# A maximum over partitions and the lower halves of weights leave GpSimd, in an mLSTM and mixture-of-experts kernel

## The chip, the cores and the metric
The kernel runs on one core of a Trainium2 chip. The time is the device time of one execution in microseconds; lower is better. An execution holds a span, from the first to the last instruction that the profiler records, and a little around it.

## The reference, cut to what matters
Three stages follow each other. The first is an mLSTM, a recurrent attention with gates, for 2 batches of 8 heads, 768 steps and heads of 40. Its output is read as 1536 rows (tokens) of 320 numbers. The second sends each row to two of eight experts and mixes their answers. The third is a two-layer network with an ELU between its layers.

```python
# first stage, for each step t
C = f_stab * C + i_stab * einsum('bhd,bhe->bhde', vt, kt)
y[:, :, t] = sigmoid(o_gate) * einsum('bhde,bhe->bhd', C, qt) / maximum(abs(nq), 1.0)
# second stage, x: (1536, 320)
noisy_logits = x @ w_gate + log1p(exp(x @ w_noise)) * noise
top2, top2_w = the two largest of a row, and their softmax
out[row] += top2_w[k] * (maximum(x[row] @ w1[e], 0.0) @ w2[e])      # w1: 8 x 320 x 1024
# third stage
h = x @ w_in                                                        # 320 x 2048, 64-bit
return where(h > 0, h, exp(minimum(h, 0)) - 1) @ w_out              # 2048 x 320, 64-bit
```

## The kernel before, in words
**Halves.** TensorE works in float16. A float32 number x is split into a high half, x rounded to float16, and a lower half, the rest x - high, also in float16; a product is then the sum of three float16 products (high by high, high by low, low by high). So every weight tile that arrives in float32 is split before use: `split_w` (line 903) makes the high half with `high` (on ScalarE for weights, `wh="A"`) and the lower half with `low`. For `low`, the entry `wl="VG"` allows two ways: one instruction on VectorE (L394), or two on GpSimd, which scale the tile in place (L392) and then subtract (L393). The weights of the last layer arrive as 64-bit numbers; `ffn_piece` (line 1053) puts float32 numbers together from their bits (L1062 to L1070) and then splits them too.

**Stages.** Attention works on 12 tiles of 128 rows, six for each batch (`attention`, `token_rows`); each tile's rows are divided by a power of two near their largest entry, kept as `inv2`, split, and written to memory. The router (`router`) runs once for each batch, with many small steps on VectorE, among them one-hot comparisons (L841, L844, L857) that TensorE sums into lists of rows (L863). For each expert and batch (`expert`), GpSimd gathers the listed rows by indirect transfers (L969), SP's queue transposes them, TensorE multiplies them with the first weights (L933), ScalarE applies the ReLU and makes the high half of the hidden rows (L988), VectorE makes the lower half (L990), and TensorE multiplies with the second weights (L946, L947, L949). Last comes the third stage on six blocks of 256 rows (`last_layer`), whose weights are fetched and split while the experts run.

**The maximum.** The third stage needs one scale for all rows. `scales` (line 1014) takes the largest entry of `inv2` in each partition (L1018), then the maximum over all partitions on GpSimd (L1019), and derives four factors from it (L1022 to L1027), which are used from the third stage on.

**The order.** All work is a list of steps, each with one or more ways (an engine and a price). A planner (`Order.plan`) once put the steps into a sequence by its own prices; the result is the table `ORDER`, which `run` decodes: for each step its number and its way. Each engine then works through its steps in that sequence, in order, and waits where a step's inputs are not there. The prices stand in the calls of `vec`, `act`, `pool` and `te` and don't change what a step does.

Of the kernel before, what the change touches and what calls it, by code (L numbers as in the profile page):

```python
# [5 lines left out]

# [63 lines left out]


ORDER = """
c-jrrzw0{hVF2*w?w<So+}(4(f8WP~gM$GB4i+2?STMzc0Sg8kEI62AieIqc;9$W)iU9)-77V<<V8MbE0|pE@7_i{rV8DVD2LlckELbpLz(D)@BVGVNfB^
>(aDV|4L<tnZ&xruUKpZrPDtHqKPy=O<0(oE%E#MGsA_<zHMWjIn0I~ooU_^X~F_8r^qC<QUUE-JIjDX~jjFS_h4%(m(dPG2QWDktV3^^wfBqFE87);3&k
pl~2N%RR!CdnD-g5Q!EVns|ygB%bka!oj7mJG-(xg#;LA<pCw6sQr{5*KnvGyo#9)Q(7#F)~Mfk$G}M?#UTBC$Hpz+!HtQP9BI1m8Xtmjw+Bv@<{wASt5^
AnS78%>I)pGI<+86)QM<Q74k`*s0-DE9grm&)Bu#J{~{(}Nv_B<)uCQwmwHoI;zGR1DVT!=sKOpqhaa*@eW)r~p;{E6t`r9WtWr1XPV}h(l_Vgw0yVNmEk
TZ`!4o_~1Rn%P)yX@RCx$$t8e{`P_zz@@Y?GL}z%9V=K|QG((Sk$DpbCTmi-bpws1DhKeRzXc_@c&CKuxF^<-iRXzyQWz8&0Va-z9tG5I%_xtkZGWg$ek9
cen!w@I@i|0cX^Um{V~g37d2Zrs2O+OA62#*q||;g(JA4TJ#tus6J`XNoqi@!35^u6h2{`x_~2a=ses|De4Qh=^2Fd3l`y)dc!mo&?B0oPoPAU;1$f_0xs
ciV28eeG5w);)SjBrfQiu?xQ26j2lsFf$`COeGvOz6oSrci_%F<qP7@1yNgv=5X1N>(nJ)cBC+HrXq`#OIouczxf+=uCuEdqO3RmSGAj#CYGpKV7uE}BM1
^RTBX>o0C3v<kvnKA>q!x_vIq?k3`<>G9bahM^UXVP?;C@@2A#&75mmuAOY0cMy9H)pm?z+~tIJLPxGf{8IlX38bmFK*1wxFWNqv-FbL(M!I>e9y0`J#z;  # L80
+I?n9rIhSG=+>%>yCHBC4z?@(4C*}<{?12Wvmd(>;_RQ4T9@po}%$h6EzvVAXh2@A1SELtwh1l>bX3s*R!B&YKTO-!Yp0Bb6p~4*LE3@TKbeV3lEw;*J*e
ttYZcL52GbjE`AK40>V=sJ-y|H=rLSN~!aHAj0iG9#__Q}+lGkam{#FlHb4W`K)*aBM=9_*8S(gUta*XR~gWM9mV@31BMz<1dm`(m$bo9VM}X272LE_3CF
?1usDi+;0j8nPXRV@K?Z|FD1?vyi*f6PDwqY)$AfeP$&5o=5DAEeUV_!vg_vUo7Tsyul8bAyW|+Y*UyB4%-p#{8%uA5o2%;7jgj`<KkSBd+>E(&Q66T>j)
_>#_qVE2`e@bp8T3^2{9qTrMV0Tg)4XCszO`1a}Vyxy|_2`;Q)W+AkPU%;CL+TxvkI_ptuvdLR`RNQCtcu0r4je^9H{c%Hlx4tivC;fak=XuoeO_CdT*-{
|g}@riCn@<MVuhFY+b6%pV0wJO~-V5H~`Fuki_?%2&js*yZD5o&ORVd`X-MC&3Zpd{g{^Fc;EdPCN@2VJl8hR`@~-AtUC5ypR%aVqVOOZ^WS=i&ZhfC;6^
;6<T6jtcg2uFV@A5I21=>Lp+F6)Z~w1Pdtfd@gk1Jr<fA@;!U`UPvIpF#Qzp1;#8a=Al=1>_!d865*f%rCG--$#Pk0*4-rCd;Ui!apcsmy3|gTNYNITA2n
n<hp)^NpltO8=K?{^ac~n3Z35ZMafV$EaEm0Nyt9V33R7SrMYp9OaVg)tO30<Tn+M&L5M~2iwjs)aAD##twMLpC<12jZEsV<Gs7!9PVG#8QFkZMv>3M5W?
pfgHJ7nG758A&avB)6rQl$QR0pd6R}7v0cC#?oEtNW7eouF_4KNExXh4W**|ke<>@!m=R;a$HWyZ)qcD<*781V)B=?lM`}U9!m=)P+I(7%4Inz@8yq_lV9
ks<fW9AW>Qi5k(5x9%0|j5DJ8|nlpY^fR?<(Txs+BiN}sRDRe2#Dq_tF68ggFRN=K<9XO*p7lUqt&DJlh}q?DDPDpjScH08S7P}<6WNCUYgx8<R{QU*#>=
_q66@07LDQ%3Sh8Y(w=B9G<1@}+d;7@jC|`Hg#WUk2(@xyui^EX|a&e2}N|Q(nk%JW_t8BykGo@kO31N4bI1IDs?xB!8(;{gU_6RnFoZF5v<$;vs&?Wn95  # L90
kyu@w%mM>hI|Ft|<YZxgT<)U1bgHp#G+{7!ng}b<i`*?!4$^cLCPWi|q{DnVwjA!_S_X<{KDo`qFPrE5|d{@rWLz&4(g;t)*0-ux(Ug0%1l{Q~jIpwSjv@
K4moLba(c#jWwEnjg<eJNG-tsL<g-|!tHY^WavV}KWGO--p?6{%^pp<ZxX#j2w=)sEWN{s+fYh<oZl?W<$;i38P9OzhyTx>F0*UX7~>^^f?VX4I=%P>*U+
&8kB+z=oF5CTdw9slQSkEzp)~hmUD-Eukf~s+Q8yT2{+x9L{S)t)LaPl2+DE>Q%d`4XvsDRI6!qEvMeqhuYH4D%Af`yQnL5t(H`*Z`6kt=pBvIN1F33ua3
2((baC+Q=4dp{?f`S(t~fYZ*y&>t+j+6)6>RNooYZ^Xz_1LEv~2al3vjr{jTNoFYTp5EvawyKdBjgrfswz>RJ7!A2m+<s6+iv+DAhg)_{I8cKSg->L-1qk
M+HtGEUl7>*`H?qF;=>{$u^DbH+u#>UVvoJ@uFV)*pIH@97`Ct@ri4Hqe35(P`tX8AesF>Bz_!L*r~rjJn>?N5;%>jKC-u*oYZZV`&tPv2i!QH%i9bSQsm
#W=!?0@ue^HjZrpoM&7s@abs=F^t!P%4qC$484Y7^9E`M?GxKKEs+bwGYyRF?>c7z|##%3!S+i)C%(~ey|JJM;RkLYs^rrDNZpO>#8gJunJdB#zGUxh5dz
u4tXmV!D_!vC{nQgOU_RKG{Z;s5d*)|NbZ%oXE88?4rzRZ~k%%zD<Xzt9pxiZ)0#ypyi`7pO;XeP|P*)e`#p3Jj(FbDj=xR_V-X1>jsnKC<8U==NB#jKK5
wklT3`k27#S`#a7VT-eR*3?3lVcqS%_0N`L)vRAw87pgztS@V3{hPJ064ug6T4QTvt*yFsww^ZUysaNvKe8HD(|Xty7dbDx>SAYO?W{l9hO@Qy*1>Y@i*>
X9Yy$^6SL<&5-a1(y>tSW=wgqg?4(zlA?TY=hURKOTcGiyDt`l=|Hnu}2VJGdX-Ej^3hj!YoxdprK*6gF*vDbFP&f7(MV#l4j{r7Iu{?2aOJ-cLg?WujTH
+I5lx@G&z?%M-<XwU7lU2sy))=oNIH{;Cgkv+B-cG~H=zqVI)!x=aiduQjZtkZIT<dmGEQ*qjE-)%X0XYZArs<U?vUfXFpHD};<oVqh~y3WuYITPpTjh%m  # L100
T=FY;II(=v9?CraEweL>CT{#D5?QEPc=a=rxIXYwach1Q<I~V8boV-ksbCWLT=G}?AbDrMWdw37$>Aak`^Kottat-(DRRZ8bcj{s{8_e8`=eS?)++Di`_w
1(J!2JvN?Z(}ryLC72%e%M>_wDW6T(Ea<-qlUJj`wT#;2zzTdvpKn9qhZC4}b@J=s(<(`*ET7bU6=sG4JKpf{YjUDqi4WuNq|BiP!ON_99GphL`kmUe?Qd
1ux+jy?L1OvTn&sdo{1>^}M=Q_WnBPdJV7S_PwU}o%fTV?fp$q52haHBj50`Kk$a$$ZPmtUO8BLWq0hQ{Iu`*fuHm<e%Ak4@bh3F#{8Tg_m^S8FZo5k;+O
rZzw!qD%xn2gKks+^RruSm?YDw<(DgTA&9D1Cf9Uu9kw5Xr{?z~8pZUjd?l1h6zx4P1+FSc~f8%w6jX(Fc;nClP2mj=s{X=;16W_M}&VTw3f9w6hfBA3!;
}gNn?*_eK5^%vF=m#(u2BY8<p2JHx4%Pt*VgU}~!8w=)v*0V(2J>JMEQ3vu2#jDK?1Ddpm*5brf?IG5uE9Nc1gBu<J%fe!4xA8#p8$qjh(a}d1-H-$V_^^
`LMMoa$uJeB!%CP5lR-Yrh1swWcEWpD4Ig1GOa=9@5st!c$VJ8QCt*2!hRyK1upI`$D@4&d{DdHa5srFcB61=l3ZhsPj|x#L>WAYn9Sy={lnydcIm$-4s2
B~RMl=cYQ7LLg?Wht}qgqstn$b8KMxAIBO`>V^eKd>a(LI`m`)Cn;h25wZfp3qfA1x#JZ5^$mXS9iq(JVYg!;t&-yJ#03qH}bKuF)-eMehiG!{0uU@$LTr
y9-B<
"""
# [1293 lines left out]
```

## Time and profile before

| | |
|---|---|
| median of 3 runs | 490.54 us (489.69 to 492.62) |
| the profiled execution | 491.45 us |
| its span | 489.1 us |
| TensorE busy | 444.3 us (91%) |
| VectorE busy | 380.3 us (78%) |
| ScalarE busy | 312.2 us (64%) |
| GpSimd busy | 164.2 us (34%) |
| mean granted clock of TensorE | 0.963 |

PE is TensorE's matrix products, PEld its weight loads, DVE VectorE, ACT ScalarE, POOL GpSimd, SP the engine whose queue starts most transfers. A letter q behind an engine's name is its sequencer. L933 is line 933 of the kernel. The granted clock is a share of TensorE's full 2.4 GHz. Matrix products overlap, so a busy TensorE need not be at its peak.

### The profile page before, as it was taken

Reading aid. Unit: us, or ns where it says so; the run is one execution under the profiler, and the core shown is the slowest. Engines: PE = TensorE matmul, PEld = TensorE weight load, DVE = VectorE, ACT = ScalarE, POOL = GpSimd, SP = SyncE. Lnnn points to the kernel's source line nnn. Section 1 sums busy time; section 2 is a strip of 40 time slices with the busy share of each in tenths; the row PEclk is TensorE's granted clock in tenths of the full one; section 3 lists DMA queues with packets and bytes.
Section 4 is the critical chain, followed back from the end, with each engine's and each line's share of the span. In section 5 each row is a group of like instructions: output and inputs, shape, how many; then the busy total and the mean of one; then the engine's idle time right before and its main releaser. Section 6 shows DMA issues by size and latency. Waiting matters only on the chain.

```text
span 489.1 us, 10625 instructions
## 1 busy us (share of the span) xinstructions
PE 444.3 (91%) x4091; PEld 374.5 (77%) x4091; DVE 380.3 (78%) x809; ACT 312.2 (64%) x522; POOL 164.2 (34%) x170
## 2 busy tenths in 40 slices
...
GB/s 144 160 142 152 240 147 139 84 220 198 211 274 232 216 243 55 167 239 248 209 222 221 259 209 102 97 102 69 39 40 56 95 15 42 55 0 28 2 28 34
DMA packets 102554, 66.43 MB, mean 136 GB/s; under 512 B 79216, under 2 KB 94112, under 8 KB 102496
## 3 DMA queue, kind: packets, MB, share of 16 engines
...
## 4 chain that ended last, share of the span: by engine, by line
PE 68%; DVE 13%; DMA 9%; issue 4%; ACT 3%; POOL 2%; SPq 1%; ACTq 0%; DVEq 0%; POOLq 0%
PE S L933 28%; PE O L946 9%; PE O L947 9%; PE O L949 8%; PE O L734 5%; DMA sf<-in_moe_w_in 2%; DMA xT<-xg 2%; PE S L667 2%; DVE hidden L990 1%; DVE one L857 1%; PE T L695 1%; PE S L677 1%; DMA sw<-in_moe_w 1%; DVE xr L394 1%; PE T L696 1%
## 5 line engine op out<-in xcount | busy, mean ns | idle before, releaser
L933 PE MATMUL S<-xT,wa 128*128 128x224 f16 (+1 forms) x1024 | 103.8, 260 | 13.8 <-DVE hidden L990 11.3
L933 PEld LDWEIGHTS <-wa 128*128 128x128 f16 x1024 | 95.2, 100 | 18.3 <-DVE hidden L990 8.8
L933 PE MATMUL S<-x3T,fwa 128*128 128x256 f16 x768 | 88.4, 273 | 2.6 <-DMA x3T<-x3r 2.6
L933 PEld LDWEIGHTS <-fwa 128*128 128x128 f16 x768 | 75.1, 98 | 13.0 <-issue 2.9
L946 PE MATMUL O<-wb,hidden 128*128 128x320 f16 (+1 forms) x256 | 75.8, 301 | 2.6 <-DVE yo L373 1.4
L947 PE MATMUL O<-wb,hidden 128*128 128x320 f16 (+1 forms) x256 | 75.7, 301 | 0.0
L949 PE MATMUL O<-wb,hidden 128*128 128x320 f16 (+1 forms) x200 | 60.4, 302 | 0.0
L946 PE MATMUL O<-fwb,gh 128*128 128x320 f16 x192 | 57.4, 299 | 0.0
L947 PE MATMUL O<-fwb,gh 128*128 128x320 f16 x192 | 57.4, 299 | 0.0
L990 DVE SCALAR_TENSOR_TENSOR hidden<-S,hidden 128x128 f16<-128x128 f32 (+2 forms) x92 | 39.7, 456 | 18.6 <-ACT hidden L988 17.4
L1146 DVE SCALAR_TENSOR_TENSOR ex<-ex,th 128x512 f32<-128x512 f32 x48 | 33.2, 691 | 22.6 <-ACT ex L1144 12.4
L969 POOL DMA_INDIRECT xg<-x_rows,table x32 | 36.7, 1145 | 38.2 <-DMA xT<-xg 21.1
L988 ACT ACTIVATE hidden<-S 128x448 f16<-128x448 f32 (+1 forms) x64 | 31.6, 512 | 16.1 <-PE S L933 13.6
L1145 ACT ACTIVATE re<-S,sca 128x512 f32<-128x512 f32 x48 | 33.0, 688 | 8.8 <-DVE gl__5584 L394 3.0
L1144 ACT ACTIVATE ex<-S,sca 128x512 f32<-128x512 f32 x48 | 32.7, 687 | 9.1 <-PE S L933 5.0
L1143 ACT ACTIVATE th<-S,sca 128x512 f32<-128x512 f32 x48 | 32.8, 687 | 8.9 <-PE S L933 8.9
...
L1147 DVE SCALAR_TENSOR_TENSOR re<-ex,re 128x512 f32<-128x512 f32 x48 | 34.0, 711 | 2.6 <-ACT re L1145 0.6
L947 PEld LDWEIGHTS <-hidden 128*128 128x128 f16 (+1 forms) x256 | 27.1, 106 | 9.8 <-issue 2.8
L946 PEld LDWEIGHTS <-hidden 128*128 128x128 f16 (+1 forms) x256 | 27.1, 106 | 7.5 <-DVE yo L1002 0.4
L383 ACT ACTIVATE gh<-re,sca 128x512 f16<-128x512 f32 x30 | 21.7, 724 | 17.2 <-DVE re L1147 17.2
L392 POOL TENSOR_SCALAR sw<-sw 128x640 f32<-128x640 f32 (+2 forms) x16 | 18.4, 1147 | 38.5 <-ACT wb L383 21.0
...
## 6 DMA issues: line engine op xcount, KB each, us to landing
...
```

Of the source, the lines that this page charges most:

```text
L933: PE.matmul(acc, wa[:, r, w, f * P:(f + 1) * P], xT[:, j, :n], start=(i == 0), stop=(i == 7))
L946: PE.matmul(o, a, wb[:, 0, f % FB], start=(f == 0), stop=False)
L947: PE.matmul(o, a, wb[:, 1, f % FB], start=False, stop=(not b and f == last))
L949: PE.matmul(o, b[0], wb[:, 0, f % FB], start=False, stop=(f == last))
L969: do([("G", 1.1, lambda: G.indirect_dma_start(out=xg()[:n], out_offset=None, in_=(x_all if hf else x_rows[0]())[:, :], in_offset=bass.Indi ...
L988: act(2 * cap, lambda: A.activation(hi(0, cap), src(0, cap), AF.Relu), [ph], [hid[f]])
L990: vec(2 * n, lambda x=x, n0=n0, n=n: V.scalar_tensor_tensor(hi(x, n), src(n0, n), 0.0, hi(n0, n), op0=OP.max, op1=OP.subtract), [ph, hid[f ...
L1143: act(512, lambda: A.activation(th(), pf(), AF.Tanh, scale=sca()[:, 2:3]), [pf, sca], [th], "exp", 1)
L1144: act(512, lambda: A.activation(ex(), pf(), AF.Exp, scale=sca()[:, 1:2]), [pf, sca], [ex], "exp", 1)
L1145: act(512, lambda: A.activation(re(), pf(), AF.Relu, scale=sca()[:, 1:2]), [pf, sca], [re], m=1)
L1146: vec(512, lambda: V.scalar_tensor_tensor(ex(), ex(), 1.0, th(), op0=OP.add, op1=OP.mult), [ex, th], [ex], port=True)
L1147: vec(512, lambda: V.scalar_tensor_tensor(re(), ex(), 0.0, re(), op0=OP.min, op1=OP.add), [ex, re], [re], port=True)
```

## The change
Three edits. The maximum over partitions is no longer one GpSimd instruction: TensorE transposes the column of 128 numbers into one row, VectorE takes the row's maximum, TensorE spreads it over the partitions by a product with a row of ones, and VectorE copies it out. The two intermediate results use the two places of memory tag T, which attention's transposes use before. The lower halves of weights have VectorE as their only way. In the planner's price of attention's float32 head products, the product with the state counts 2 x 128 columns instead of 128. The table is new.

```diff
-    kq="A", yo="VA", wh="A", hv="VA", wl="VG", q3l="V")
+    kq="A", yo="VA", wh="A", hv="VA", wl="V", q3l="V")
...
 ORDER = """
-c-jrrzw0{hVF2*w?w<So+}(4(f8WP~gM$GB4i+2?STMzc0Sg8kEI62AieIqc;9$W)iU9)-77V<<V8MbE0|pE@7_i{rV8DVD2LlckELbpLz(D)@BVGVNfB^
...
+c-jrtJIeyyfdJq$_cQnV%$b=p^BS<QFkoR}zz<xourOd@VPU|+1q-uSSQzjF0~Qt*2HeGf0SgNY0|pFO7;wP_7YtY!aKV6u1Pd1|TyWw2VE6eI4*)dK00a
...
+    def ps_f():
+        return buf(lambda: psum, [P, 512], F32, "T", 2, turns=False)
...
-        n, cols = ((3 + (c > 0)) * H, P) if halves else (H, 4 * P + P * (c > 0))
+        n, cols = ((3 + (c > 0)) * H, P) if halves else (H, 4 * P + 2 * P * (c > 0))
...
-        mb = Buf(lambda: None)
+        mb, mt_ = Buf(lambda: None), Buf(lambda: None)
+        m2 = route.tile([P, 1], F32, name="m2")
+        pm, pb = ps_f(), ps_f()
         vec(12, lambda: V.tensor_reduce(m1, inv2(), axis=AX.X, op=OP.max), [inv2], [mb])
-        pool(1000, lambda: G.partition_all_reduce(smax(), m1, P, bass_isa.ReduceOp.max), [mb], [smax])
+        te(1, 4 * P, lambda: PE.transpose(pm()[:1, :P], m1, id32()), [mb], [pm])
+        vec(P, lambda: V.tensor_reduce(m2[:1], pm()[:1, :P], axis=AX.X, op=OP.max), [pm], [mt_])
+        te(1, P, lambda: PE.matmul(pb()[:, :1], ones32()[:1, :], m2[:1], start=True, stop=True), [mt_], [pb])
+        vec(1, lambda: V.tensor_copy(smax(), pb()[:, :1]), [pb], [smax])
```

Decoded, the two tables compare as follows. The steps rise from 1995 to 1998: VectorE's from 772 to 796, TensorE's from 348 to 350; ScalarE keeps 517 and SP's queue 224; GpSimd's fall from 134 to 111. Twenty-two lower halves of weights move from GpSimd to VectorE, 16 of expert weights and 6 of the last layer's. Of the last layer's roundings, 17 move from ScalarE to VectorE and 8 the other way; of the copies of experts' results, 10 move from VectorE to ScalarE and 6 the other way; three multiplies of last-layer weights move from VectorE to GpSimd. The sequence of experts and batches on TensorE is the same, but the steps of neighbours interleave in another way, and nearly every step stands at another place. In the new table the transpose comes right behind the first product step of expert 3, batch 0; VectorE's maximum 107 VectorE steps behind the step that feeds the transpose; the product that spreads it 46 TensorE steps behind the transpose, among expert 5; the copy among expert 7.

## Rows read from the trace of the kernel before

**Rows 1.** The page's head and busy time: us, share of the span, instructions.
```profile
span 489.1 us, 10625 instructions
...
PE 444.3 (91%) x4091; PEld 374.5 (77%) x4091; DVE 380.3 (78%) x809; ACT 312.2 (64%) x522; POOL 164.2 (34%) x170
```
**Rows 2.** Busy us by stretch, then clock, DMA share, GB/s; experts and last layer.
```profile
130.00:305.00 175.00, 159.15 (x1402) 137.42 (x1400) 140.57 (x258) 100.06 (x178) 67.92 (x59) 0.97 0.81 207
...
321.00:484.00 163.00, 162.24 (x1344) 131.43 (x1344) 121.70 (x204) 112.80 (x189) 23.52 (x25) 1.00 0.16 40
```
**Rows 3.** The chain that ended last, around and behind the maximum: start, us, what.
```profile
184.79 7.03 issue
191.82 1.26 POOL nm L378
...
203.64 2.87 POOL wb L393
...
207.04 5.79 DMA sf<-in_moe_w_in
```
**Rows 4.** Instructions of the maximum's line: min/median/max ns, first and last start.
```profile
L1019 POOLq MODIFY_POOL_CONFIG  x2: 13/13/13, 177.5 to 177.5; - x2
L1019 POOL PARTITION_ALL_REDUCE smax<-m x1: 378/378/378, 184.3 to 184.3; - x1
```
**Rows 5.** Waits from 176 to 200 us: total us, times, longest.
```profile
DVE hidden L990 <- ACT hidden L988: 11.3, 1, 11.3
ACT fwa L383 <- POOL nm L378: 11.1, 1, 11.1
...
POOL smax L1019 <- DMA sw<-in_moe_w: 6.8, 1, 6.8
```
**Rows 6.** TensorE's waits over the whole run, the longest.
```profile
PE S L933 <- DVE hidden L990: 11.3, 5, 8.0
```
**Rows 7.** Busy us by stretch, as rows 2, behind the maximum.
```profile
192.00:200.00 8.00, 5.17 (x25) 3.70 (x26) 5.47 (x8) 5.82 (x9) 6.75 (x6) 0.50 0.22 55
208.00:220.00 12.00, 8.94 (x83) 7.50 (x82) 10.12 (x22) 5.75 (x11) 3.51 (x3) 1.00 1.13 241
```
**Rows 8.** Instructions of two lines near to the new ones, as rows 4.
```profile
L516 PE MATMUL O<-lf,ones x2: 423/476/529, 8.4 to 8.8; 128*128 128x96 f32 x2
...
L1018 DVE TENSOR_REDUCE m<-inv x1: 150/150/150, 178.0 to 178.0; 128x1 f32<-128x12 f32 x1
```
**Rows 9.** Lower halves of weights on GpSimd and on VectorE, as rows 4.
```profile
L392 POOL TENSOR_SCALAR sw<-sw x16: 737/1037/2437, 65.2 to 285.7; 128x640 f32<-128x640 f32 x7, 128x1024 f32<-128x1024 f32 x5, 128x960 f32<-128x960 f32 x4
L392 POOL TENSOR_SCALAR nm<-nm x6: 458/536/630, 194.4 to 298.4; 128x320 f32<-128x320 f32 x5, 128x512 f32<-128x512 f32 x1
...
L394 DVE SCALAR_TENSOR_TENSOR wa<-sw,wa x19: 1208/1218/3149, 64.5 to 279.3; 128x1024 f16<-128x1024 f32 x19
L394 DVE SCALAR_TENSOR_TENSOR wb<-sw,wb x13: 821/1153/1937, 89.3 to 285.0; 128x960 f16<-128x960 f32 x12, 128x640 f16<-128x640 f32 x1
...
L394 DVE SCALAR_TENSOR_TENSOR fwb<-nm,fwb x11: 481/491/493, 219.7 to 306.9; 128x320 f16<-128x320 f32 x11
```
**Rows 10.** Busy us by stretch, as rows 2, where the router's steps fill VectorE.
```profile
64.00:76.00 12.00, 6.84 (x81) 6.08 (x81) 12.00 (x22) 9.78 (x15) 8.28 (x6) 0.78 0.59 147
94.00:104.00 10.00, 6.77 (x89) 6.04 (x88) 9.80 (x24) 5.69 (x9) 8.59 (x8) 0.87 0.76 166
113.00:122.00 9.00, 5.87 (x61) 4.57 (x59) 8.69 (x15) 4.65 (x6) 5.44 (x4) 0.99 0.68 173
```
**Rows 11.** VectorE instructions there: busy us and mean ns, else as rows 4.
```profile
L857 DVE TENSOR_TENSOR one<-minus,bs 128x512 f16<-128x512 f16 x6 | 7.6, 1326 | 0.0
...
L857 DVE TENSOR_TENSOR one<-minus,bs x6: 678/1072/2489, 70.1 to 120.5; 128x512 f16<-128x512 f16 x6
...
L841 DVE TENSOR_TENSOR rh<-starts,as x3: 348/1186/1564, 65.7 to 114.8; 128x192 f16<-128x192 f32 x3
...
L394 DVE SCALAR_TENSOR_TENSOR xr<-yb,sc,xr x24: 239/468/2026, 30.0 to 103.2; 128x256 f16<-128x256 f32 x12, 128x64 f16<-128x64 f32 x12
```

More of the change, by code (lines that the diff above doesn't have):

```diff
@@ L8 @@
 import concourse.tile as tile
-from concourse import bass_isa, mybir
+from concourse import mybir
 from concourse._compat import with_exitstack
@@ L72 @@
 ORDER = """
-c-jrrzw0{hVF2*w?w<So+}(4(f8WP~gM$GB4i+2?STMzc0Sg8kEI62AieIqc;9$W)iU9)-77V<<V8MbE0|pE@7_i{rV8DVD2LlckELbpLz(D)@BVGVNfB^
[L74 to L107, printed above, removed]
@@ L108 @@
-y9-B<
+c-jrtJIeyyfdJq$_cQnV%$b=p^BS<QFkoR}zz<xourOd@VPU|+1q-uSSQzjF0~Qt*2HeGf0SgNY0|pFO7;wP_7YtY!aKV6u1Pd1|TyWw2VE6eI4*)dK00a
+_1pahzP1u%$#I7opaXb=ga3d#TzHSi%4AVwrXi)ev1Q3rW2BGMoO0NDhHD1Z(zBf7*-L=Ql6Owi<<$bupHJF-VCh$RsxE1(M!WE+ftL}bVbF(o9@BKpLN(
+1;vJ5gM5!Epkna$t*b_a%6^@kZEE^4v8swAv45`+z?wLPwt2mIRuEDlY25v?ujee2RUj%9*6_k07vpj+{i4Ir#b+Wck)5T$P=+4k5qvyP(^A0o@AETl0|X
+`mSl;lQ!nyNoyarMrjkU7ER!c{MgEO!P*d<<M1>rK3w0$rRF!;_YqCsz$S&2SKGcn<P!FO;ev?)DO0}pQF$X=WPu0n9Y7J^Mpc*7i)#)3x0u36{O&ZX5YC
+zHSgQ`*!umClxKtM{OG)kg1`c5yw9$55~xX@?%U&tXfqAaRNJgFAlBF~^l=ZP1!0}~!mSGr9jx<ikt7}clS<bdvyH~K|<({F0ZZ$X23&^>ZOVXDsDL7ci1
@@ new lines @@
+nC{X?5Thk#NMAvRoKhPAm^Yy@BRWne=p;R(p0vfxsTR{@64Z-cP$_y$e=})%LeKdO9VeF5ibBi@Wa%lrrurn!%;+4wr3NHqlGL0YF*_<n<!Q{!nHxw`3wl
+Yf=sk6y#>}7THnXKSbdi36H@#qDOo^7*Jw0X#woF%O$bRSpm@o(WNT299v!SL;7Um$$PT4t|U{-vG=`u^E$IO@{lZORZge6#p6L!U<m<mj=8oOqyum<a}0
+h_P|vuvLMM3NmaGqw#outcPpH^{LTo8Y$mkU{K*>B1q*vm==1Fgu1Rw!jwI1-oN2%o9xDmPv70W(s#qoQtt(cE{61fj+TGZU%Sso;kA%e$Vc>GBJl4cFA5
+qiH)-dX2$231<W%mb_JJk4IiMy6_^jWum`rx7MUZv=F8lbt*||K;Okt2D>D`D8yuM`x8$pAAJ*6!w`QB%hTroCuEkY|Ew|?~T$QM^ZSKaNm@Kz}Ij+KN*b
+;MRPuv!snHq8CA8c8;@OQ4tK;pujxh;F+8*G!ka5W~+U6}%RWA4m@Yq1aJ!9Upnyz?)%&33pWSLEu%o9%Kv?!)%EZ}!PuxfeI!ZXDpA%$s}iAFj(Dd79h7
@@ new lines @@
+E8k&Xe4nidkUR0;9Dp>0uqM2iH#6iUZp4kb4`Xo>oN#;i<~7)32keKp;E)}$2m+xgOgY41I2GpHjH?SBffg{g<f=j(#^8!;2{8c*F)j($Tnf&GZ(b5+!iH
+-IX_$ds;Rf46Pq@Pee8Lxe!w>w1fTwxLOT5O#1x>I7jZX*`pAru62>Zf9K>SuXLClYYfiM(u!cNe{7@y&>m=u=6O33mHZZ9CABIfu!kA(tX<gY?rDDi9IA
+dH2CxDjHaC8mX%m=qJR%uj?0kHjip<Bvj0jElbzPQp!i3Uxj$cKN%I5gU9}tcxA-A!NmZkQ0kSQOt`+u`8a1xwMonLQgCS1+g!_#D!E68{$f`q?6bbFXC0
+ai7oM4$O>n%EM}yaFcITC5C`J_2vhMc&cwF(Ez<Hse2Q}sNN@2YR;3<KOA8T7LvbXIMM;*VwX~CBk|rSuOCKRFF=9`;NJ}vx{ak|LM%qhT3CbzyAZhYI-i
+UcAEfu7qbd<8vpTwM0lFE`KHl(dMlIwCsx=Kyy-^IOHlUh<;YVvKVBi*E-)RoraNxDlJIV&H;vow;%(p&0FmOPLq(omjCEg8u<c_uaFw%n9EGM2k?Paex3
@@ new lines @@
+=^@4BxSW(9vZNrTtR&>P^54=+O380|D{D$sIVfp)F6ZT+q_SL)E6PX4N?-n#ck)xVl$4TCV#-TS@JT+a)ReTcmlyI$DJV$=C>bT8<`i04%0)S^ROFSsmN)
+W5p2|?E%0+c1C)KpNQ8Q{*tt)-Lp){42(pEZ3OD!rXwWPGwqw-H`MJ>sBwW_xGj#^NG+*J>9U%AL*<tU$(fihG|YFQnqJGHCyl&gG_*Gf&T$rEL&^wfV=h
+w4bV$up&|j?`}@#ix0oo?%0sD;H&<Y?PNWR%a@$PSm;DRF`T}o2pl3rEb-|x=`=RP047qp3=_pMNMn*uadS_vszBeYi(_!{ZZK}lKxf-+C%v$MQy1+m9kd
+Rs#;CkDF^kTUe%il)w_IDkt(Tmt)VqFsQ0wB-qJc+SKDd>{-)j4zBbT?+DIE~bM2&lRIDzvr#jVU+DkpFD@9j-rfT}Py3|(MT6?Q?{h%GSmA=t-8qknt>3
+a=oEq!Rv+DY3hXRV=k^^4ZllX^y%G^`=Lsb96H_R`|&Mo;M--BQN}*6&(Re`^E%p=I^Hu4`lcXIfhSU+r6)=`lU7SIn4^(~o*Wx3r-?(zp6kk82ZsuIKfH
@@ new lines @@
+HZe~6$N>6FKkFC0X1?{Ze$@+lMc?UrJ!vfTl=0E0dfJE^2_s`<jhu1N^G3-i7{AoZM#X3tPorp5jhp@}y=F8V&1@ST<F40@rg4E?1Dg+BGFrxOjfL?srpC
+9f89QUhTP89~IxrGu%=|W%#>(g$17l{?&7=v;s#()tM#_8}j4?NCBW|Y6oVhm+1~M|%+8CG{V{2s0qj5DRX3;#FCxbCN=Fq$uISZPSnKduw$;?_e>ug@lv
+U4-<CN!pI-pZRL^JV_c7@1@93Lj>{w5*5qG`nWmoS74=VK&X4+2-eF-+Y^Qt7W#$Z}Vx@th@35;jo(4!rYhz>tTG%xwW#OwKbP!%#tk4idzZmVjv4!b*o{
+Ot(Nt+rxrHa*1{@UTWe-5t+iFL4%WshS${Hj*2~(Nd-H51zLH-#yK1e?pIa#_ZSAeM^|9)9(T4W7b+JnJ(Yjh43)p%4U`lqu9`R*+V0EpNRk1C*YPamR-L
+VID%^q4y`?uD&P1_B-X?JbSMt01`cF*qHLwjtW?B7`<d(5ZozBRF@_ROB!8+&1|?6tkM<Mz(p+hglsr|pk@w9hthG$&#I!ls?1owYCa)xOzx`(Z!rmtAqH
@@ new lines @@
+PR;2%b;oiN4sw!C*MZK!k({|Rbg;8<Qcl{5IU}d({Hrr{;?C0fy|Z%u>};KlGjn!M-g&zPC*$m$ADnOZ?i`(uYoUXK5I_y@<j^igE$8f9oQLyt{_eb-7?R
+wZ^L9G?$ANCnvD}{=&5gSZ%Dcc#x^cv#gquKhH|-)f<z`&${@@nfy&H4e&M%$5n{%&j!Ie<MO`?)pb}McQ4cwMnbvw@7y}1Xs?$z9;+jfWU*d4hOx8rtQ4
+gJAwda19z*K=oX%UieuZ|U}&G%BN&+eUZy=$4$ew|0N@GHBygP{+%nJj$UeDxkl(MYMD4sEf{i33X5(^}HHtprO}81Jp!gH1ht<`@Ppf5BKD*(ZxTzQ#3>
+)G(mGTLko2E|KM%W27UY`+MyMCx_fj+7j#8;bn_4Bh92mMX5JIM{WtoD|BYTK?OEOj6+Psg5cYr<^Y&iJd-`+l;@-WCM|;qVdk;V1efzRk_Of2m%j1Q&^w
+yr{9lVrx^v>SO+jtKT1Sjv}74X*Ed4Kn4Kj+2$r}y%1-rM_lKY4T@`I;{UFaUlXLthIlANipl^Amp3Px)y-?^nEnpYiK{-!J(^zw9^tyjR38zk!>$;s4<0
```

5 lines of the change are left out of this document (added).

## The prediction
> **What bounds the kernel now.** I read the page's busy line first: TensorE is busy 444.3 of 489.1 us, VectorE 380.3, GpSimd only 164.2 [rows 1]. TensorE is the engine to watch, and the question is where its missing 45 us lie. The busy time by stretch answers it: from 321 to 484 us, the last layer, TensorE works 162.24 of 163.00 us, while from 130 to 305 us, the experts, it works 159.15 of 175.00, so nearly 16 us are missing there [rows 2]. Nothing done to the other engines can shorten the last layer; a hole before it moves the end one for one.
>
> The chain of waits names the largest hole. It runs through GpSimd: behind the maximum over partitions 7.03 us pass, from 184.79 us on, with nothing to wait for, and only then a plain multiply of weights starts, at 191.82 [rows 3]. The instructions of the maximum's line show two changes of GpSimd's loaded code, both at 177.5 us, and the maximum itself, of 378 ns, only at 184.3 [rows 4]. The table of waits gives 6.8 us idle before the maximum, which it puts down to a transfer of expert weights [rows 5]; the maximum reads no such weights, so I take it for the load of the code, with the second gap as the load back. GpSimd thus does one 0.38 us instruction in the 14.3 us from 177.5 to 191.82. The waits show who stands behind it: ScalarE waits 11.1 us for the multiply, and as ScalarE works in order, its ReLU of an expert waits too; VectorE idles 11.3 us behind that ReLU [rows 5]; TensorE idles 8.0 us in one piece behind VectorE [rows 6]. From 192 to 200 us TensorE then runs at a granted clock of 0.50, the lower of its two levels, 1.2 GHz [rows 7].
>
> By the Trainium skill, "GPSIMD Engine Reference", section 2.1 Instruction dispatch, the first call of a freshly loaded GpSimd kernel pays about 6 us for loading code, with no instruction of its own in the profile. The trace agrees as far as its first gap goes; two such loads would be an estimated 11.9 us by that page, against gaps of 6.8 and 7.03 us here.
>
> **The maximum, part by part.** *Removed:* the GpSimd instruction and its block. Term A is TensorE's 8.0 us of idle time [rows 6]. Term B is the slow clock behind it: 5.17 us of work between 192 and 200 us, all of it at half clock [rows 7], would have taken half, so 2.6 us. Term C is the echo: from 208 to 220 us TensorE misses 12.00 - 8.94 = 3.1 us [rows 7]. The chain there still runs through GpSimd, which finishes a late lower half at 203.64 + 2.87 us, and through the transfer of last-layer weights that follows it, 5.79 us from 207.04 on [rows 3]. I take the 3.1 us as returned, since that half leaves GpSimd too; bounds 0 and 3.1. With the hole and its echo gone, nothing on this chain is late any more but TensorE's own products.
>
> *Added:* a transpose and a one-row product on TensorE, a maximum and a copy on VectorE. The nearest row is a float32 product against a matrix of ones, two instructions of 423 to 529 ns [rows 8], for 96 columns; the new ones have 128 and 1. Two pairs cost at most 2.1 us and at least nothing, if they fall into idle time; I take 0.7 us, a third of the bound, since one of the two moves a single column and the instructions of a pair overlap. The maximum over 12 columns took 0.15 us on VectorE [rows 8]; the two new VectorE instructions are of that size, and VectorE has 175.00 - 140.57 = 34 us free in the experts' stretch [rows 2]. If that cover were gone they would cost 0.3 to 0.5 us. As for new waits: in the new table VectorE's maximum stands 107 of its steps behind the one that feeds the transpose, the broadcast product 46 TensorE steps behind the transpose, and the consumer far behind both, so nothing should queue behind a wait. If one did wait, the next expert's products would stand behind it on TensorE.
>
> **Lower halves of weights, from GpSimd to VectorE.** GpSimd does 16 halves of expert weights (7 of 640 columns, 5 of 1024, 4 of 960) and 6 of last-layer weights [rows 9]. On VectorE the same step takes 1.218 us for 1024 columns, 1.153 for 960, 0.82 for 640 (the least of that row), and 0.491 for the last layer's of 320 [rows 9] (one of the six has 512 columns and costs a little more). The sum: 5 x 1.218 + 4 x 1.153 + 7 x 0.82 + 6 x 0.491 = 19.4 us more on VectorE. Where they lie decides.
>
> Six of them (three of 1024, one of 960, two of 640) lie in the three stretches where the router's steps keep VectorE full: 12.00 of 12, 9.80 of 10 and 8.69 of 9 us, with TensorE at 6.84, 6.77 and 5.87, so 11.5 us idle [rows 10]. They add 6.45 us to VectorE. But VectorE is slow there because GpSimd works beside it: the one-hot comparison (L857) takes 1326 ns on average and 678 at best, L841 takes 348, 1186 and 1564 ns, and the lower half of a token row took up to 2026 ns against a median of 468 [rows 11]. Against their shortest durations the excess is 6 x 0.648 + (1.186 + 1.564 - 2 x 0.348) + 1.56 = 7.5 us. By the Trainium skill, "SBUF — State Buffer", section Who interferes with whom, a VectorE instruction with two inputs from SBUF and a GpSimd instruction that reads SBUF hold each other up entirely, by order of issue. The trace agrees: the slow ones are such instructions. Term D is then a relief of 7.5 - 6.45, some 1 us. The bounds are a relief of all 7.5 us, if the new order finds room for the six elsewhere, and a loss of 6.45, if something else stretches those instructions.
>
> The other sixteen, 12.9 us, go into VectorE's 34 us of free time; TensorE's own queue of ready work hides them, and I cost them at nothing. Without that cover they delay the step that hands an expert's hidden rows on.
>
> **Order anew.** The longer float32 price is an entry in the planner's arithmetic and issues no instruction; it acts through the table alone. The table keeps the sequence of experts, goes from the experts to the last layer by the same eight steps of the last expert and six of the first block, and issues the same 224 steps on SP's queue. In the last layer nine more roundings go to VectorE, which has 163.00 - 121.70 = 41 us free there under a full TensorE [rows 2]: nothing. Three more multiplies go to GpSimd, whose steps fall from 134 to 111: nothing. All else is reshuffled at places that I can't price; I hold this at 0, with a few us either way.
>
> **The sum.** -8.0 - 2.6 - 3.1 - 1.0 + 0.7 = -14.0 us. The profiled execution took 491.45 us, its span plus 2.35; it gives 477.4. The median of the runs shown is 0.9 us lower, 490.54, and gives 476.5. I say 477.
>
> **Rivals.**
> *The gift is partly spent.* The block goes (A and B, 10.6 us), but the sixteen lower halves outside the router stand ahead of hidden rows on VectorE, and half of their 12.9 us lands on TensorE: 491.45 - 10.6 + 0.7 + 6.5 = 488 without C, 485 with it. For it: VectorE works in order, and TensorE already waits on that step. Against it: outside the hole that wait is small, 11.3 us in five waits of which one is the hole's 8.0 [rows 6]. Chance 0.16.
>
> *VectorE becomes the bound, slower than before.* All 19.4 us land on TensorE's path, with no relief in the router's stretches: 491.45 - 10.6 + 0.7 + 19.4 = 501 us. It decides from the point at which more than half of them, 9.9 us, is not hidden. For it: VectorE is full in the three router stretches. Against it: 12.9 of the 19.4 fall where it has 34 us free. Chance 0.06.
>
> *The change doesn't free what it seems to.* The gaps around the maximum belong to the weight transfer and to something the profile doesn't show, and only 0.38 us of GpSimd's time goes while TensorE pays 0.7: 491 to 492 us. For it: the releaser named in the profile. Against it: the two code loads on that line, and the second gap, released by nothing. The Trainium skill, "GPSIMD Engine Reference", section 4.1 Engine selection, sends a reduction along partitions to GpSimd, which speaks against this edit; the two gaps in the rows speak for it. Chance 0.05.
>
> The forecast has the remaining 0.73.
>
> **Numbers.** A measurement of this kernel tells about 1% from no change, 4.9 us. Faster by over 1% (below 485.6) takes the forecast and half of the first rival: 0.81. Within 1%, the other half and the third rival: 0.13. Slower by over 1%: 0.06. Low end: A, B, C and the full relief make -21.2, so 470, and 2 us for the order: 468. High end: 487, inside the first rival; the other two stay out.
>
> **What would show it.** After: no maximum and no code load on GpSimd; no stretch near 190 us with all engines idle; granted clock 1.0 there; the last layer starting some 14 us earlier with its 163 us unchanged; VectorE busy near 400 us less the relief, GpSimd well below 164 us; L857 near 0.7 us. I am wrong if TensorE's waits for VectorE's hidden rows grow by more than 5 us, if a new hole of several us opens before the last layer, or if the router's stretches lengthen.

## The result and the profile after

The changed kernel takes 470.62 us (median of 4 runs, 468.79 to 473.07), the kernel before beside it 491.06 (4 runs, 489.69 to 492.62). The ratio is 0.9586 [0.9532, 0.964]: 20.4 us faster, where 14 were forecast. Ratios leave out one run, of "both, old order" below at 474.81 us, that came out in a slower state of the chip. The profiled execution of after took 473.07 us, 18.4 less than that of before.

The page of after, its head and busy time (us, share of the span, instructions), answers [rows 1]:

```profile
span 471.4 us, 10570 instructions
...
PE 439.8 (93%) x4094; PEld 371.2 (79%) x4094; DVE 374.6 (79%) x833; ACT 310.3 (66%) x522; POOL 114.7 (24%) x125
```

TensorE's busy time hardly changes; the span shrinks around it. VectorE is to be noticed: it does 24 more instructions, 22 lower halves among them, and is busy 5.7 us less.

Busy us by stretch in after, columns as in [rows 2]: the experts, two stretches that answer [rows 7], the last layer, and the three router stretches that answer [rows 10]:

```profile
130.00:305.00 175.00, 166.86 (x1482) 145.95 (x1481) 137.67 (x281) 105.19 (x191) 39.98 (x39) 0.99 0.82 215
192.00:200.00 8.00, 7.25 (x79) 6.88 (x78) 6.10 (x12) 4.56 (x9) 2.47 (x2) 1.00 1.11 295
208.00:220.00 12.00, 12.00 (x109) 10.40 (x107) 9.33 (x19) 8.13 (x16) 1.02 (x2) 1.00 0.95 230
303.00:466.00 163.00, 162.24 (x1344) 131.44 (x1344) 124.74 (x216) 108.17 (x182) 28.64 (x27) 1.00 0.17 41
64.00:76.00 12.00, 10.40 (x129) 8.53 (x127) 12.00 (x33) 11.12 (x18) 5.65 (x4) 1.00 0.50 112
94.00:104.00 10.00, 5.94 (x75) 5.40 (x73) 7.25 (x16) 7.16 (x12) 3.00 (x4) 0.81 0.86 224
113.00:122.00 9.00, 8.85 (x94) 7.34 (x92) 9.00 (x16) 5.70 (x8) 1.27 (x1) 1.00 0.68 179
```

The hole at 190 us and the half clock behind it are gone, and from 208 to 220 us TensorE has no gap. The last layer takes the same 163 us and starts 18 us earlier (at 303.05 instead of 321.01 us). So the whole gain was made before it, one for one.

TensorE's waits in after (total us, times, longest), against [rows 6]:

```profile
PE bank L639 <- ACT xTt L373: 3.9, 2, 2.7
PE S L935 <- DMA xT<-xg: 3.5, 3, 2.1
...
PE S L935 <- DVE hidden L992: 1.2, 2, 0.6
```

The wait for VectorE's hidden rows fell from 11.3 to 1.2 us. Nothing took its place at that size.

**When the time came.** I placed each kernel against before by the expert products that it had issued up to a moment, each counted once: each first product at 0.096 us and each of the second products of one line at 0.405 us (16 of the first took 1.53 us in a stretch without gaps; three lines at 0.135). The lead over before, in us, worked out so from the traces:

```
                        130    160    184    200    220    300 us
after                   7.2    0.2    3.1   13.7   16.9   16.7
after, run again        8.0    5.3    8.4   18.5   21.4   17.7
maximum only            0.0    0.2    0.0    9.9   10.5    9.1
lower halves only       4.4    4.2    4.5   11.1   13.4   12.6
both, old order         6.8    6.3    9.6   18.5   22.1   17.3
six early halves        2.3    2.6    3.1    4.8    3.4    4.0
sixteen late halves    -1.2   -1.6    0.9    5.9    6.7    7.4
```

Two executions of one kernel differ by up to 5 us in such a row, as the first two show. Still the shape is plain: about 7 us are won before 130, some or all of them are given back by 160, some 10 come from 184 to 200 (10.6 and 10.1) and 3 from 200 to 220 (3.2 and 2.9). One flaw is new in after: from 130 to 160 us it gives back 7.0 us (2.7 when run again). Its chain there (start, us, what) is a transfer of transposed rows that takes 8.43 us:

```profile
138.44 8.43 DMA xT<-xg
146.88 0.14 issue
147.01 2.33 PE S L935 x16
```

"Both, old order" gives back 0.5 there and its time can't be told from that of after, so the loss makes no difference that I can show.

### The profile page after: what moved, and what is told of

It is laid out like the page before. It is cut to its first block, busy times and chain, and to the rows that moved or that the text cites. A ratio compares the mean times of both kernels' runs of the same rounds, so it can differ in the third digit from the quotient of the medians.

```text
span 471.4 us, 10570 instructions
## 1 busy us (share of the span) xinstructions
PE 439.8 (93%) x4094; PEld 371.2 (79%) x4094; DVE 374.6 (79%) x833; ACT 310.3 (66%) x522; POOL 114.7 (24%) x125
## 4 chain that ended last, share of the span: by engine, by line
PE 72%; DVE 12%; DMA 8%; ACT 3%; issue 2%; another core or an unknown queue 1%; SPq 0%; ACTq 0%; DVEq 0%
PE S L935 32%; PE O L948 10%; PE O L949 10%; PE O L951 9%; PE O L736 3%; DMA xT<-xg 2%; DMA sw<-in_moe_w 2%; DVE wa L393 1%; DMA xg<-x_rows,table 1%; DVE hidden L992 1%; DMA sf<-in_moe_w_in 1%; PE S L669 1%; PE T L697 1%; DVE wb L393 1%
## 5 line engine op out<-in xcount | busy, mean ns | idle before, releaser
L935 PE MATMUL S<-xT,wa 128*128 128x224 f16 (+1 forms) x1024 | 100.6, 256 | 6.4 <-DMA xT<-xg 3.5
L935 PEld LDWEIGHTS <-wa 128*128 128x128 f16 x1024 | 93.5, 99 | 10.2 <-issue 5.5
L971 POOL DMA_INDIRECT xg<-x_rows,table x32 | 35.4, 1107 | 66.9 <-DMA xT<-xg 36.7
L1153 DVE SCALAR_TENSOR_TENSOR ex<-ex,th 128x512 f32<-128x512 f32 x48 | 33.1, 693 | 18.7 <-ACT th L1150 12.9
L393 DVE SCALAR_TENSOR_TENSOR wa<-sw,wa 128x1024 f16<-128x1024 f32 x24 | 29.0, 1224 | 2.8 <-ACT wa L382 2.8
L736 PE MATMUL O<-vw,pw 128*128 128x120 f32 x176 | 28.7, 305 | 0.4 <-POOL pw L706 0.4
```

Of the source, the lines that this page charges most:

```text
L393: some(on, [("V", 0.07 + 0.06 * m + 1.04e-3 * n, lambda: V.scalar_tensor_tensor(dst(), src(), scale(), hi(), op0=OP.mult, op1=OP.subtract) ...
L736: PE.matmul(po()[:, h * D1:h * D1 + WIDE], pw()[:, h], vw_()[:, h * D1:h * D1 + WIDE], start=True, stop=not c)
L935: PE.matmul(acc, wa[:, r, w, f * P:(f + 1) * P], xT[:, j, :n], start=(i == 0), stop=(i == 7))
L971: do([("G", 1.1, lambda: G.indirect_dma_start(out=xg()[:n], out_offset=None, in_=(x_all if hf else x_rows[0]())[:, :], in_offset=bass.Indi ...
L1153: vec(512, lambda: V.scalar_tensor_tensor(ex(), ex(), 1.0, th(), op0=OP.add, op1=OP.mult), [ex, th], [ex], port=True)
```

## The experiments

Three edits make the change, so I undid and did them separately. Each ratio is against the kernel before, beside it on the same chip. "Old order" means the table of before; there the four new steps of the maximum have no places, so the kernel emits them at fixed steps of that table.

**The maximum alone, old order.**

```diff
-        pool(1000, lambda: G.partition_all_reduce(smax(), m1, P, bass_isa.ReduceOp.max), [mb], [smax])
+            pool(1000, lambda: None, [mb], [smax])
+            EXTRA.update({918: one, 1047: two, 1197: three, 1332: four})
```

> The kernel before with its own order, the lower halves still on GpSimd; only the maximum goes through TensorE and VectorE, its four steps put at the places near which they stand in the changed kernel. Theory (the code loads around GpSimd's maximum block GpSimd, and through it ScalarE, VectorE and TensorE): no stretch with all engines idle near 190 us, and 10.6 to 14 us gained, 477 to 480 us. Rival (the new order is what gains): 488 to 491 us.

484.19 us, 0.9848 [0.9766, 0.9929]: 7.3 us faster, short of the 10.6 expected. GpSimd's multiply now starts at 182.25 us instead of 191.82, and the busy time of 184 to 200 us shows TensorE at full clock:

```profile
182.25 1.26 POOL L382 TENSOR_TENSOR nm<-nm,na 128x512 f32<-128x512 f32 x1 [5.14 <-DMA sw<-in_moe_w]
...
184.00:200.00 16.00, 14.55 (x139) 12.85 (x138) 11.76 (x18) 9.89 (x17) 11.06 (x9) 1.00 0.70 183
```

Before was busy 7.98 us in the same stretch, at 0.69. TensorE's 8.0 us hole is gone, and the lead won from 184 to 200 us is 9.9 us, close to the 10.6 of terms A and B; 0.6 us follows by 220. Some 1.4 of it are given back by 300, and the profiled span is 7.8 us shorter. One new wait is TensorE's for the transpose's input at 177.9 us, 1.5 us. The mechanism holds in its place; less than the whole of it reaches the end.

**The lower halves alone, old order, maximum still on GpSimd.**

```diff
-        low(n, lo, x, lambda: scale, hi, [*r, w], [w], on=ON["wl"])
+        f = lambda: V.scalar_tensor_tensor(lo(), x(), scale, hi(), op0=OP.mult, op1=OP.subtract)
+        do([("V", 0.07 + 1.04e-3 * n, f, True)] * 2, [*r, w], [w])
```

> The kernel before with its own order and GpSimd's maximum; only the 22 lower halves go to VectorE, at the places where they stood. Theory of the prediction: the hole stays, the router's stretches get about 1 us, the other halves are hidden: 488 to 490 us. Rival (VectorE was held up by GpSimd in the experts' stretch too): 3 to 7 us gained, 484 to 488 us. Rival (VectorE becomes the bound): 495 us or more.

477.43 us, 0.9711 [0.9625, 0.9797]: 14.1 us faster, more than any of the three expectations. The prediction gave this part 1 us; here it failed. GpSimd's order of work in this kernel (start, us, instruction, idle before it and what ended it):

```profile
159.99 1.82 POOL L970 DMA_INDIRECT xg<-x_rows,table  x1 [7.64 <-DMA xT<-xg]
170.82 0.75 POOL L1020 PARTITION_ALL_REDUCE smax<-m  x1 [9.01 <-DVE m L1019]
179.59 1.25 POOL L378 TENSOR_TENSOR nm<-nm,na 128x512 f32<-128x512 f32 x1 [8.01 <-issue]
```

Its waits from 160 to 205 us show what is left of the cost:

```profile
ACT fwa L383 <- POOL nm L378: 6.4, 1, 6.4
PE O L947 <- DVE yo L373: 4.0, 2, 3.5
```

The block around the maximum lasts 17.8 us here, from the gather's end to the multiply, longer than the 14.3 of before (the maximum waits for its input until 170.7 us). But it begins at 161.8 us instead of 177.5 [rows 4], because the three halves that stood ahead of it are gone, and ScalarE waits 6.4 instead of 11.1 us.

**Both, old order; and the changed kernel with the maximum back on GpSimd, new order.** The second edit:

```diff
-        te(1, 4 * P, lambda: PE.transpose(pm()[:1, :P], m1, id32()), [mb], [pm])
...
+        pool(1000, lambda: G.partition_all_reduce(smax(), m1, P, bass_isa.ReduceOp.max), [mb], [smax, pm])
```

> Both edits in the order of before. Theory (the two edits add up, the new order gives nothing): 470 to 472 us, as the changed kernel. Theory of the prediction with its own sizes: 476 to 477 us, the rest of the changed kernel's gain being the order's. Rival (the old order wastes it): 480 us or more.

> The changed kernel with the maximum back as one GpSimd instruction, at the place of the transpose, in front of a multiply of last-layer weights. Theory (block): a hole of some 8 us on TensorE near 180 us, low clock behind it, 8 to 14 us lost, 479 to 485 us, with 6 to 7 us on both sides of the maximum on GpSimd. Rival (only the old order stood badly around it): 471 to 474 us.

Both in the old order: 469.06 us, 0.9514 [0.9435, 0.9594]; the table brings nothing that shows. The changed kernel with GpSimd's maximum: 469.95, 0.956 [0.9496, 0.9624], no slower than after, against my theory of 479 to 485. The block is in it all the same. GpSimd's rows there:

```profile
160.34 1.50 POOL L971 DMA_INDIRECT xg<-x_rows,table  x1 [8.40 <-DMA xT<-xg]
170.23 0.38 POOL L1023 PARTITION_ALL_REDUCE smax<-m  x1 [8.40 <-issue]
177.53 1.26 POOL L377 TENSOR_TENSOR nm<-nm,na 128x512 f32<-128x512 f32 x1 [6.92 <-issue]
```

15.7 us pass between the gather's end and the multiply, more than in before (14.3), and both gaps end by "issue": the profile names no transfer behind them. Why it costs nothing is seen in ScalarE's timeline in the same kernel:

```profile
167.99 0.54 ACT L990 ACTIVATE hidden<-S 128x448 f16<-128x448 f32 x1 [0.46 <-PE S L935]
...
174.02 1.06 ACT L382 ACTIVATE wa<-sw 128x1024 f16<-128x1024 f32 x1
178.82 0.63 ACT L382 ACTIVATE fwa<-nm 128x512 f16<-128x512 f32 x1 [3.75 <-POOL nm L377]
179.36 0.47 ACT L990 ACTIVATE hidden<-S 128x384 f16<-128x384 f32 x1
```

and in that of before, at the same place:

```profile
181.26 0.72 ACT L1063 ACTIVATE nm<-nm,edge 128x512 f32<-128x512 f32 x1
193.11 0.63 ACT L383 ACTIVATE fwa<-nm 128x512 f16<-128x512 f32 x1 [11.13 <-POOL nm L378]
193.64 0.47 ACT L988 ACTIVATE hidden<-S 128x384 f16<-128x384 f32 x1
```

In before, ScalarE came to the late multiply 11.13 us too soon and had an expert's ReLU right behind it. In the experiment it does ReLUs and roundings all through the block and waits 3.75 us; TensorE's largest waits from 160 to 205 us are 1.7 and 1.6. So the cost of the block here went by what stood in the queues that waited for it, and not by its length.

**The halves split in two.** In the old order with GpSimd's maximum, only the six halves in the router's stretches go to VectorE, or only the sixteen others:

```diff
+        if do.main and len(do.ops) in EARLY:
+            f = lambda: V.scalar_tensor_tensor(lo(), x(), scale, hi(), op0=OP.mult, op1=OP.subtract)
+            do([("V", 0.07 + 1.04e-3 * n, f, True)] * 2, [*r, w], [w])
+        else:
...
```

> The kernel before with its own order and maximum; only the first six lower halves, those of the router's stretches, go to VectorE. Theory (there GpSimd holds up VectorE, so TensorE idles and its clock falls): some 5 us ahead by 130 us and kept to the end, 485 to 487 us. Rival (what the lower halves gave came from GpSimd's lateness at the maximum): 489 to 492 us.

> The kernel before with its own order and maximum; the other sixteen lower halves go to VectorE, the first six stay on GpSimd. Theory (without four halves between 160 and 178 us GpSimd reaches the maximum earlier and loads its code while nobody waits): nothing gained by 160 us, 7 to 9 us gained around 190 us, 481 to 484 us. Rival (all the gain is in the router's stretches): 489 to 492 us. The prediction's own cost for these sixteen was nothing.

Six early: 487.05 us, 0.9876 [0.9839, 0.9914], 5.1 faster over the runs, 3.0 in its profiled execution. Sixteen late: 482.88, 0.9822 [0.977, 0.9875], 9.3 faster. Together 14.4, as both at once (14.1). With the six moved, the hole at 190 us is untouched: ScalarE's 11.1 and TensorE's 8.0 us stand in its waits as in [rows 5, 6]. With the sixteen moved, its waits from 160 to 205 us read

```profile
ACT fwa L386 <- POOL nm L381: 8.0, 1, 8.0
...
PE S L940 <- DVE hidden L997: 3.4, 1, 3.4
```

so TensorE's hole shrank from 8.0 to 3.4 us, though the maximum is still GpSimd's. VectorE's busy time tells the rest. The pages' lines of busy time, first of the six, then of the sixteen:

```profile
PE 447.1 (92%) x4091; PEld 376.7 (77%) x4091; DVE 373.2 (77%) x815; ACT 312.7 (64%) x522; POOL 153.1 (31%) x158
```

```profile
PE 444.4 (92%) x4091; PEld 374.7 (78%) x4091; DVE 377.7 (78%) x825; ACT 312.0 (65%) x522; POOL 127.1 (26%) x138
```

With 6.45 us of halves added (the sum of [rows 9] durations), VectorE is busy 7.1 us less than the 380.3 of before: its other work shrank by 13.6 us. With 12.9 added it is 2.6 less: 15.5.

**New order with neither edit, and with the maximum alone.** The changed kernel with both undone, and with only the 22 halves put back on GpSimd:

```diff
-        low(n, lo, x, lambda: scale, hi, [*r, w], [w], on=ON["wl"])
+        low(n, lo, x, lambda: scale, hi, [*r, w], [w], on="G" if do.main and len(do.ops) in GPS else ON["wl"])
```

> The changed kernel's order with both edits undone: the maximum on GpSimd at the place of the transpose, the same 22 lower halves on GpSimd. Theory (the edits do it, not the order): 487 to 495 us, as before. Rival (the new order itself gains): 470 to 480 us.

> The changed kernel with only the 22 lower halves back on GpSimd; the maximum stays on TensorE and VectorE. Theory (the lower halves are the larger part, some 13 us): 481 to 486 us. Rival (the maximum is the larger part, as the prediction had it): 472 to 476 us.

Neither: 492.09 us, 1.0007 [0.9969, 1.0044]. The maximum alone: 477.76, 0.9747 [0.9678, 0.9817], between the two ranges expected: in this order it is worth 14.4 us by itself. In the kernel with neither edit the block comes late again, and ScalarE waits 13.5 us for the multiply and TensorE 12.5 in one piece.

**Does a GpSimd that reads hold VectorE up?** To the kernel with both edits in the old order I gave idle work on GpSimd, at the places where the six early halves stood: once operations that read constants from SBUF, once fills that only write. Their results are used by nobody.

```diff
+                for _ in range(n // 256):
+                    G.tensor_scalar(z, cau, scale, 0.0, op0=OP.mult, op1=OP.add)
+                for _ in range(n // 256):
+                    G.tensor_tensor(z, cau, on_, op=OP.subtract)
```

```diff
+                for _ in range(3 * (n // 256)):
+                    G.memset(scr16, 1.0)
```

> Both edits in the order of before, and at the six early places GpSimd does idle work besides: after the high half is there, as many columns of two-input and one-input instructions as it had, in pieces of 256 columns, on constants, with a result that nobody reads. Theory (GpSimd instructions that read SBUF hold up VectorE): the one-hot comparison above 0.8 us again and 2 to 6 us lost against both edits alone, 471 to 476 us. Rival (what counted was the data's way through GpSimd): no loss, 468 to 470 us.

> As e9, but GpSimd's idle work only writes (fills, three for each pair). Theory (reading holds up VectorE, writing doesn't): the one-hot comparison at 0.68 us, no loss, 468 to 470 us. Rival (any GpSimd work there delays GpSimd's own next steps): as much lost as in e9.

Reads: 478.02 us, 0.973 [0.9693, 0.9767]; fills: 467.97, 0.9522 [0.9489, 0.9556]; the same kernel without either 471.45, 0.9572 [0.9535, 0.9608]. The groups of instructions (busy us, mean ns, idle before), with reads:

```profile
L929 POOL TENSOR_TENSOR scr<-causal,ones 128x256 f16<-128x256 f32 x19 | 18.0, 948 | 1.5
...
L927 POOL TENSOR_SCALAR scr<-causal 128x256 f16<-128x256 f32 x19 | 14.1, 740 | 1.6
...
L867 DVE TENSOR_TENSOR one<-minus,bs 128x512 f16<-128x512 f16 x6 | 4.5, 791 | 0.0
```

and with fills:

```profile
L924 POOL MEMSET scr<- 128x256 f16 x57 | 17.8, 312 | 3.3
...
L867 DVE TENSOR_TENSOR one<-minus,bs 128x512 f16<-128x512 f16 x6 | 3.8, 678 | 0.0
```

From 64 to 130 us, busy us by stretch as above, the kernel without idle work, then the one with reads, then the one with fills:

```profile
64.00:130.00 66.00, 54.83 (x580) 47.33 (x579) 58.30 (x160) 43.42 (x68) 24.69 (x20) 0.90 0.71 180
```

```profile
64.00:130.00 66.00, 52.69 (x520) 46.20 (x520) 58.80 (x144) 39.03 (x61) 51.94 (x63) 0.82 0.60 157
```

```profile
64.00:130.00 66.00, 56.04 (x588) 47.72 (x586) 58.22 (x162) 44.52 (x70) 42.45 (x83) 0.90 0.72 181
```

The pages' busy time, with reads and then with fills:

```profile
PE 445.2 (93%) x4094; PEld 376.5 (79%) x4094; DVE 380.8 (80%) x833; ACT 311.7 (65%) x522; POOL 142.8 (30%) x169
```

```profile
PE 442.0 (94%) x4094; PEld 372.9 (79%) x4094; DVE 373.4 (79%) x833; ACT 311.9 (66%) x522; POOL 130.2 (28%) x188
```

GpSimd's busy time rises by 18.6 us with fills, and nothing is lost; VectorE's one-hot comparison keeps its 678 ns. With reads VectorE gets through 144 instructions in this stretch instead of 160, TensorE through 520 instead of 580, and 6.6 us are lost against the kernel without idle work, somewhat more than expected. VectorE's same 833 instructions are busy 380.8 us with reads, against 374.3 without and 373.4 with fills: 6.5 us more beside a GpSimd that reads, none beside one that fills. By the Trainium skill, "SBUF — State Buffer", section Who interferes with whom, a VectorE instruction with two inputs from SBUF contends with a GpSimd instruction that reads, and not with one that only writes; these busy times agree. The comparison alone says little: its mean of 791 against 678 ns is one of six at 1152, the others at some 0.68 us. GpSimd's side shows something like it. The fills took 17.8 us, about what the six halves took in before (18.0, the sum of their rows), so that much GpSimd work by itself cost nothing; the reads took 32.1 us, though by their shortest durations, 403 and 667 ns, they would have taken 20.3:

```profile
L927 POOL TENSOR_SCALAR scr<-causal x19: 403/406/2832, 66.1 to 120.5; 128x256 f16<-128x256 f32 x19
```

I read the rest as GpSimd held up in turn; that is inferred from these durations alone. It makes GpSimd late (TensorE waits 2.1 us once for a mask step of GpSimd's), and how the 6.6 us divide between VectorE held up and GpSimd late stays open.

**The order again.** The kernel with both edits in the old order, and the changed kernel itself, beside each other:

> Both edits in the order of before, again, beside the changed kernel. If the new order gives something, this is slower than the changed kernel; the theory so far: the same or up to 2 us faster, 468 to 471 us.

> The changed kernel again, for the comparison with e11: 469 to 472 us.

471.45 us, 0.9572 [0.9535, 0.9608], and 470.43, 0.9559 [0.9525, 0.9593]. With both edits, as with neither, the order makes no difference that can be measured. The eight combinations, as ratios:

```
                       old order           new order
neither                1                   1.0007
maximum alone          0.9848              0.9747
lower halves alone     0.9711              0.956
both                   0.9514, 0.9572      0.9586, 0.9559
```

In the old order the two edits add up: 7.3 and 14.1 us alone, 20.0 and 22.5 together. In the new order they overlap: 2.6 and 4.5 hundredths of the time alone, 4.2 to 4.5 together. With the lower halves alone the order does count (0.9711 and 0.956, with intervals that just don't meet): TensorE's longest wait from 160 to 205 us is 3.5 us in the old order and 1.7 in the new.

## Why the prediction was right, and which terms were off

**What bounds the kernel.** Right. The last layer kept its 163 us, and a hole before it moved the end one for one.

**A and B, hole and slow clock.** Right in mechanism and place, and near in size: 10.6 us were forecast; the maximum alone won 9.9 between 184 and 200 us, the changed kernel 10.6. The granted clock there is 1.00 now. But with the maximum alone in the old order only 7.3 us reached the end, where A and B less the added steps made 9.9.

**C, the echo.** 3.1 us forecast, 3.2 won from 200 to 220 in after, 0.6 with the maximum alone. With the lower halves alone it is 2.3, with both in the old order 3.6: it returns, but in full only where the halves have left too, as forecast.

**D, the relief in the router's stretches.** Mis-sized: 1 us forecast, 5.1 by the six early halves (4.2 to 7.9 by the interval of the ratio at 492.16 us for before), and a lead of 2.3 to 8.0 us at 130 us in the kernels of the table with these halves moved. That a GpSimd which reads holds VectorE up is borne out by the reads and the fills, and the bound of 7.5 holds the result, but I added up three lines only: 7.5 us of VectorE's time, where 13.6 came free. The lines that I did count came out near their shortest durations, as in after's rows (min/median/max ns), which answer [rows 11]:

```profile
L859 DVE TENSOR_TENSOR one<-minus,bs x6: 670/678/685, 70.1 to 117.2; 128x512 f16<-128x512 f16 x6
...
L393 DVE SCALAR_TENSOR_TENSOR xr<-yb,sc,xr x24: 267/450/1071, 30.1 to 96.2; 128x64 f16<-128x64 f32 x12, 128x256 f16<-128x256 f32 x12
```

I also put no price on the clock in those stretches. From 72 to 84 us TensorE ran at half clock in before and at full clock in after; before, then after:

```profile
72.00:84.00 12.00, 8.90 (x70) 7.81 (x69) 8.43 (x22) 4.43 (x9) 5.15 (x6) 0.50 0.50 139
```

```profile
72.00:84.00 12.00, 9.47 (x109) 7.65 (x108) 11.93 (x33) 8.34 (x15) 7.82 (x6) 1.00 0.52 135
```

That is 8.90 / 2 = 4.5 us by the working of term B. It isn't a firm part of the gain, though: with the six early halves moved the clock there was still 0.59, and with fills 0.57, and the fills' kernel ended as early as any.

**The sixteen late halves at nothing.** Wrong, and the largest miss: 9.3 us by themselves. VectorE showed no new wait for them, as forecast. What I did not follow was the other side, GpSimd rid of them. Three of them stood shortly ahead of the maximum on GpSimd's queue, the last of them ending at 177.5 us; without them the block begins 10.1 us earlier (at 167.4 us; 15.7 earlier with all 22 moved), and more of it overlaps with work that ScalarE has anyway. The lead row agrees: 5.0 of its 7.4 us come from 184 to 200, where the hole was. The rest isn't explained: VectorE's other work also shrank by 15.5 us here, and no run moves only the three halves ahead of the maximum, which would separate the two. So A and B can be had in two ways, by taking the maximum away or by bringing GpSimd to it in time, and the prediction gave the first the credit for both. In the new order, with the halves moved, taking the maximum off GpSimd is worth nothing (0.956 against 0.9586 and 0.9559); in the old order it is still worth 1.4 to 2.0 hundredths of the time (0.9711 against 0.9572 and 0.9514, the first with a wide interval).

**The added steps.** The new path takes 0.27 us for the transpose, 2 x 0.26 for the spreading product, 0.27 and 0.15 on VectorE; 0.8 on TensorE and 0.4 on VectorE, against 0.7 and 0.3 to 0.5 forecast. Nobody waits for any of them:

```profile
L1023 PE MATMUL T<-id,m x1: 273/273/273, 173.7 to 173.7; 128*1 128x128 f32 x1
L1024 DVE TENSOR_REDUCE m<-T x1: 271/271/271, 203.7 to 203.7; 1x1 f32<-1x128 f32 x1
L1025 PE MATMUL T<-m,ones x2: 245/256/266, 241.2 to 241.3; 1*128 1x1 f32 x2
L1026 DVE COPY smax<-T x1: 151/151/151, 273.9 to 273.9; 128x1 f32<-128x1 f32 x1
```

**Order anew at 0.** Right for the change as it is: 1.0007 [0.9969, 1.0044] with both edits undone, and no difference with both done. It does decide how the gain divides between the two edits.

**The rivals.** *VectorE becomes the bound* fell: VectorE is busy 374.6 us and not "near 400 less the relief"; the relief was 25.8 us in the old order with all halves moved (373.9 busy, 19.4 added, against 380.3). *The gift is partly spent* fell in its mechanism: the wait for hidden rows went down to 1.2 us. *The change doesn't free what it seems to* fell with the maximum alone taken away, which took the hole with it, and with the kernel in which both gaps end by "issue"; but its second half, that taking the maximum away alone could be worth little, came true in the new order once the halves had left.

**The sum.** -14.0 had the right sign, and the range held the result, but it was 6 us short: D lacked some 4, and the late halves were at nothing where they gave 9.3 by themselves. That it came as near as that is partly luck: in the old order the maximum alone gave 7.3 us where 9.9 were set down for it (13.0 with C), and the lower halves alone 14.1 where 1.0 was set down (4.1 with C). What stays open: why after loses 7.0 us (2.7 when run again) between 130 and 160 us (no kernel changed that transfer), and how much of the relief before 130 us is the clock's.
